# Interleaving two hidden units of a dense layer with chunk attention on one Trainium2 core

## Chip, cores and metric

The kernel runs on one core of one Trainium2 chip. The metric is the time of one execution on the device in microseconds (us), as the median of several runs. Before the change three runs took 1961.25, 1962.05 and 1965.11 us.

## What is computed

Three stages follow each other. Everything is float32; only shapes and the operations matter here.

```python
# 1. chunk attention: batch 4, heads 8, sequence 576, head size 64, chunks of 64
scores = q_c @ k_c.T / sqrt(64); attn = softmax(scores); x = attn @ v_c
x = x.transpose(0, 2, 1, 3).reshape(2304, 512)
# 2. dense layer ("first layer"): w_in 512x2048, w_out 2048x512 (float64 inputs)
h = x @ w_in; g = s * relu(h)**2 + b; x = g @ w_out
# 3. mixture of 8 experts with a doubly normalised gate
P = exp(x @ w_gate - max); P = normalise rows and columns of P, 8 times
out = sum over e of P[:, e] * (relu(x @ w1[e]) @ w2[e])
```

## The kernel before

**Tokens.** The 2304 tokens are 18 tiles of 128, numbered from 0, in 6 groups of 3 tiles (`GT`). Attention works by tile. The first layer works by group, so its products have 384 columns.

**Attention.** `attn_stages(t)` is a generator with five steps for a tile t. Step 0 transposes q and k on TensorE (banks `pq`, `pk`; 4 transposes each), ScalarE copies them to `qT` and `kT`, and the loads of tile t + 3 are issued on SyncE's queue. Step 1 makes the scores (`sc`, two banks, 32 small matmuls); VectorE takes the row maximum (`mx`) and subtracts it (into `pr`, or into spare room of the tile `whole`). Step 2 is the softmax: ScalarE's exp (L284), three VectorE instructions for the reciprocal of the row sums (`sm`, L286 to L288), and GpSimd's product (L289). Step 3 transposes the result (`pa`), and ScalarE copies it to `aT`. Step 4 multiplies by v (`px`, two banks); ScalarE writes the high part `xTh` of the layer's input and VectorE the low part `xTl`; the v of tile t + 2 is loaded. `attention()` runs the steps as a pipeline over tiles: in one round tile r has step 0, tile r - 2 step 2, tile r - 1 step 1, tile r - 3 step 3 and tile r - 4 step 4. A call of `stage()` advances it by one step (step 2 comes along with the next).

**First layer.** The 2048 hidden columns are 8 units of 256. For unit u and group g, `up1(u, g)` makes h: for each of two halves f, 12 matmuls of 128x384 into a bank `ph` (`three` sums high x high, high x low and low x high over 4 blocks of rows). ScalarE then does relu to `r` (L359), VectorE squares (L361), ScalarE writes the high part `gh` (L365), and VectorE the low part `gl` (L340), which `later()` puts off by one half. `down1(u, g)` makes the unit's share of the output: 4 slices of 6 matmuls into banks `po`. For unit 0 ScalarE copies the slice to the accumulator (L390); for other units VectorE adds it (L392). I write U(u, g) and D(u, g) for the two. All PSUM banks come from one ring of 8, in the order of the code.

**Weights.** They are float64 in memory, and are rounded to float32 and split on the chip, in blocks of 512 KB: a unit has blocks 4u and 4u + 1 (w_in) and 4u + 2 and 4u + 3 (w_out). `convert(i)` is two ScalarE instructions on the raw words (L189, L190), three on VectorE (L191, L193, L197) and two on GpSimd (L200, L201). `finish(i)` merges on VectorE (L208), writes the high part `wh` on ScalarE (L213) and the low part `wl` on GpSimd (L214). The generator `unit_conversion` alternates: convert(i), then finish(i - 1) with the load of raw block i + 1. There are two raw buffers (blocks 2 and 3 lie in spare room). Unit u's weights lie in a buffer of the pools `wpa` or `wpb`, by turns.

**Order.** The code writes the order out by hand, and each engine takes its own instructions in that order. While attention runs, unit 0 alone is interleaved with it: three attention steps stand behind each product slice (`stage(3)`), and as many as are missing stand ahead of each group (`while done[0] < ...: stage()`). The rest of unit 0's conversion is written in one piece behind U(0, 0). D of a group is written behind U of the next. When attention is through, the remaining slices of unit 0 and then units 1 to 7 follow, with the next unit's conversion beside each.

```python
                if u == 0:
                    while done[0] < G0[g] + GT[g]:
                        stage()
                    side = lambda: stage(3)
```

## Time and profile before

| what | value |
|---|---|
| three runs | 1961.25, 1962.05, 1965.11 us; median 1962.05 |
| span of the profiled execution | 1964.4 us; of the three runs only the one of 1965.11 us is longer |
| TensorE busy | 1917.2 us, 98% of the span |
| VectorE, ScalarE, GpSimd busy | 1377.4, 982.9, 156.4 us |
| TensorE busy in the first three of 40 slices | 6, 8 and 8 tenths; GpSimd works in the first ten slices only |

TensorE is busy nearly all the time, so most of the time is work that the change leaves alone. Attention and most of unit 0 lie in the first 127 us. Within that stretch one reads the idle time of TensorE, what ended it, and the granted clock.

### The profile page before, as it was taken

How to read it: one execution, taken by the hardware profiler on the slowest of the kernel's cores; microseconds unless marked ns; L12 is line 12 of the kernel's file. 1: busy time of each engine (PE TensorE's matmuls, PEld its weight loads, DVE VectorE, ACT ScalarE, POOL GpSimd, SP SyncE). 2: the span in 40 equal slices, each digit the busy share in tenths (PEclk: the TensorE clock that was granted, in tenths of full speed). 3: DMA queues.
4: the chain of work that ended last, by engine and by line, in shares of the span. 5: the costliest groups of instructions: out<-in, count | busy, mean ns of one | idle time of the engine just before them, and what ended most of it. 6: DMA issues, size and time to landing. Idle time of an engine off the chain costs nothing.

```text
span 1964.4 us, 34768 instructions
## 1 busy us (share of the span) xinstructions
PE 1917.2 (98%) x13859; PEld 1889.7 (96%) x13859; DVE 1377.4 (70%) x2417; ACT 982.9 (50%) x1793; POOL 156.4 (8%) x126
## 2 busy tenths in 40 slices
PE   6889999999899999999999999999999999999999
PEld 5779999999799999999999999999999999999998
DVE  5666777775767666656665666888887878788775
ACT  4664333335544445454545444555555555555553
POOL 4333333330000000000000000000000000000000
PEclk9899999999999999999999999999999999999999
DMA  8521111100155565556555656867676766767675
GB/s 193 144 65 43 44 44 43 44 22 12 39 201 212 197 227 220 205 204 225 222 204 205 225 222 226 295 188 226 178 229 189 224 200 205 223 190 226 180 228 168
DMA packets 295729, 335.71 MB, mean 171 GB/s; under 512 B 65936, under 2 KB 254352, under 8 KB 295568
## 3 DMA queue, kind: packets, MB, share of 16 engines
q1 hardware_dynamic: 295568, 333.50, 52.1%
q8 instruction: 108, 1.77, 0.4%
q14 instruction: 53, 0.43, 0.1%
HBM read 196.63 MB, written 136.84 MB: 170 GB/s over the span
## 4 chain that ended last, share of the span: by engine, by line
PE 90%; DVE 4%; ACT 3%; issue 1%; DMA 1%; POOL 0%; SPq 0%; DVEq 0%; ACTq 0%; POOLq 0%
PE wb L612 71%; PE ph L107 9%; PE po L107 9%; DVE sm L286 0%; DMA vs<-in_v_dram 0%; DVE mx L279 0%; ACT whole L660 0%; DVE whole L280 0%; DVE x L521 0%; ACT r L369 0%; DMA whole<-in_q_dram 0%; PE px L304 0%; ACT r L359 0%; DVE xs L524 0%; ACT r L368 0%
## 5 line engine op out<-in xcount | busy, mean ns | idle before, releaser
L612 PEld LDWEIGHTS wb<-x,x 128*128 128x128 f32 x6048 | 726.1, 192 | 2.4 <-ACT wb L850 2.2
L612 PE MATMUL wb<-x,x 128*128 128x256 f32 x6048 | 726.8, 283 | 1.5 <-ACT wb L850 1.5
L612 PE MATMUL wb<-x,w1h 128*128 128x384 f32 x2688 | 686.8, 337 | 6.9 <-ACT w1h L572 2.2
L612 PEld LDWEIGHTS wb<-x,w1h 128*128 128x128 f32 x2688 | 484.5, 188 | 10.1 <-ACT wb L687 3.2
L612 PE MATMUL wb<-x,w1l 128*128 128x384 f32 x1344 | 451.8, 336 | 0.1
L817 DVE TENSOR_TENSOR x<-st,x 128x1024 fp32r<-128x1024 f32 (+1 forms) x288 | 308.3, 1089 | 101.7 <-ACT x L816 100.3
L816 ACT ACTIVATE x<-st 128x1024 fp32r<-128x1024 f32 (+1 forms) x288 | 272.1, 945 | 111.3 <-issue 79.4
L612 PEld LDWEIGHTS wb<-x,w1l 128*128 128x128 f32 x1344 | 252.7, 188 | 0.4 <-DVE w1l L574 0.4
L844 DVE SCALAR_TENSOR_TENSOR whole<-wb,lg,whole 128x256 f32<-128x256 f32 (+1 forms) x333 | 166.0, 530 | 49.2 <-PE wb L612 46.7
L850 ACT ACTIVATE wb<-wb 128x256 f32<-128x256 f32 x216 | 79.4, 368 | 233.1 <-PE wb L612 221.8
L675 DVE SCALAR_TENSOR_TENSOR whole<-wb,whole 128x384 f32<-128x384 f32 x192 | 98.1, 552 | 126.8 <-PE wb L612 105.4
L660 ACT ACTIVATE whole<-whole 128x384 f32<-128x384 f32 x192 | 100.2, 527 | 156.1 <-DVE whole L666 118.5
L107 PE MATMUL po<-gh,wh 128*128 128x384 f32 x384 | 130.8, 341 | 1.4 <-ACT whole L390 0.8
L107 PE MATMUL ph<-xTh,wh 128*128 128x384 f32 x384 | 130.1, 339 | 0.8 <-ACT xTh L312 0.8
L107 PE MATMUL ph<-xTl,wh 128*128 128x384 f32 x384 | 129.4, 337 | 1.3 <-DVE xTl L313 1.3
L107 PE MATMUL ph<-xTh,wl 128*128 128x384 f32 x384 | 129.4, 337 | 0.0
L107 PE MATMUL po<-gl,wh 128*128 128x384 f32 x384 | 128.9, 336 | 0.0
L107 PE MATMUL po<-gh,wl 128*128 128x384 f32 x384 | 128.8, 335 | 0.0
L361 DVE SCALAR_TENSOR_TENSOR r<-r,s_bc 128x384 f32<-128x384 f32 x84 | 64.7, 770 | 75.4 <-ACT r L359 75.4
L574 DVE TENSOR_TENSOR w1l<-w,w1h 128x512 fp32r<-128x512 f32 (+1 forms) x128 | 79.0, 620 | 34.3 <-ACT w1h L572 34.3
L365 ACT ACTIVATE gh<-r,b_bc 128x384 fp32r<-128x384 f32 x84 | 51.9, 617 | 82.6 <-DVE r L361 82.6
L692 ACT ACTIVATE whole<-wb 128x384 f32<-128x384 f32 x96 | 47.4, 494 | 91.2 <-PE wb L612 91.1
(133 smaller groups left out, 1974.1 us busy)
## 6 DMA issues: line engine op xcount, KB each, us to landing
h<-whole SPq DMA_DIRECT2D x96, 1344.0 KB, 5.7
st<-h SPq DMA_DIRECT2D x216, 512.0 KB, 4.5
w<-in_moe_w_dram SPq DMA_DIRECT2D x60, 512.0 KB, 6.8
st<-h SPq DMA_DIRECT2D x72, 256.0 KB, 4.3
raw<-in_moe_w_in_dram SPq DMA_DIRECT2D x16, 512.0 KB, 3.6
raw<-in_moe_w_out_dram SPq DMA_DIRECT2D x14, 512.0 KB, 3.5
vs<-in_v_dram SPq DMA_DIRECT2D x72, 64.0 KB, 2.6
out_dram<-whole SPq DMA_DIRECT2D x18, 256.0 KB, 3.9
```

The costliest lines, as they stand in the source:

```text
L107: nc.tensor.matmul(out, lhsT=x, rhs=y, start=(i == 0), stop=(i == n - 1))
L361: nc.vector.scalar_tensor_tensor(out=r, in0=r, scalar=s_bc[:, 0:1], in1=r, op0=ALU.mult, op1=ALU.mult)
L365: nc.scalar.activation(out=hh, in_=r, func=AF.Identity, bias=b_bc[:, 0:1])
L574: nc.vector.tensor_tensor(out=dst(lo), in0=src, in1=dst(hi).bitcast(F32), op=ALU.subtract)
L612: nc.tensor.matmul(out, lhsT=x, rhs=y, start=fresh and i == 0, stop=i == n - 1, skip_group_check=True)
L660: nc.scalar.activation(out=dst, in_=src, func=AF.Relu)
L675: nc.vector.scalar_tensor_tensor(out=dst, in0=view(b), scalar=0.0, in1=y, op0=ALU.max, op1=op)
L692: nc.scalar.activation(out=u2, in_=b, func=AF.Copy)
L816: nc.scalar.activation(out=h, in_=src, func=AF.Copy)
L817: nc.vector.tensor_tensor(out=l, in0=src, in1=h.bitcast(F32), op=ALU.subtract)
L844: nc.vector.scalar_tensor_tensor(out=dst, in0=src, scalar=g, in1=dst, op0=ALU.mult, op1=ALU.add)
L850: nc.scalar.activation(out=dst, in_=src, func=AF.Copy)
```

## The change

- Units 0 and 1 both run on a group as it leaves attention. The order of the slices is now a list (`steps`): U(0,0), D(0,0), U(0,1), U(1,0), D(0,1), U(0,2), D(1,0), U(1,1), D(0,2), U(0,3), D(1,1) and so on, to D(1,4); D(1,5) follows with unit 2.
- Attention steps are spread evenly: 12 between two groups, over the slices that lie there (`pending`): two steps behind each slice of the first group, later one.
- Blocks 0 to 11 (units 0 to 2) are converted beside attention, at places that a table (`turns`) names by slice. Behind the first half of U(0,0) it has two turns in one: finish(2) with the load of raw block 4, and convert(4).
- D(0,0) comes directly behind U(0,0); `flush()` writes the low parts that it needs ahead of it.
- The weight buffers are opened once. A third one (`wc`) holds the w_in part of units 2 and 5, and is closed ahead of unit 6.
- Units 2 to 7 run as before.

```diff
--- before.py
+++ after.py
@@ -59,6 +59,8 @@
     xp = [None] * NG
     for g in reversed(range(NG)):
         xp[g] = open_pool(x_stacks[g], f"xp{g}")
+    third = ExitStack()
+    wc = open_pool(third, "wc", bufs=2)
     cv = open_pool(early, "cv", side="right")
     at = open_pool(early, "at", bufs=2, side="right")
     ffn_banks = ExitStack()
@@ -136,10 +138,15 @@
                 )
 
 
+    pairs = [[p.tile([P, 2, KD * UN], F32R, tag="w", name=f"w{x}{i}") for x in "hl"]
+             for i, p in enumerate(wp)]
+    ups = [[t[:, 0] for t in both] for both in pairs]
+    ups.append([wc.tile([P, KD * UN], F32R, tag="w", name=f"wc{x}") for x in "hl"])
+    dns = [[t[:, 1] for t in both] for both in pairs]
+
     def part_tiles(u):
-        both = [wp[u % 2].tile([P, 2, KD * UN], F32R, tag="w", name=f"w{x}{u}") for x in "hl"]
-        up = [t[:, 0].rearrange("p (k f) -> p k f", k=KD) for t in both]
-        dn = [t[:, 1].rearrange("p (k f) -> p k f", k=UF) for t in both]
+        up = [t.rearrange("p (k f) -> p k f", k=KD) for t in ups[u % 3]]
+        dn = [t.rearrange("p (k f) -> p k f", k=UF) for t in dns[u % 2]]
         return up, dn
 
     units = []
@@ -213,9 +220,8 @@
         nc.scalar.activation(out=dh, in_=m, func=AF.Copy)
         nc.gpsimd.tensor_tensor(out=dl, in0=m, in1=dh.bitcast(F32), op=ALU.subtract)
 
-    def unit_conversion(first):
-
-        n = len(conv)
+    def conversion(first, n):
+
         load_raw(first)
         load_raw(first + 1)
         yield
@@ -886,7 +892,8 @@
         load_qk(0)
         make_identity(nc, ident)
         nc.gpsimd.memset(ones, 1.0)
-        plan_unit(0)
+        for u in range(NU1):
+            plan_unit(u)
         load_raw(0)
         load_qk(1)
         load_raw(1)
@@ -913,7 +920,7 @@
                 if x is not None:
                     done[0] = x
 
-        cg = unit_conversion(0)
+        cg = conversion(0, 12)
         next(cg)
         i = 0
         while done[0] < GT[0]:
@@ -922,7 +929,59 @@
             stage()
             i += 1
         stage(2)
-        prev = None
+
+        def flush():
+            while lows:
+                later()
+
+        steps = [("U", 0, 0), ("D", 0, 0), ("U", 0, 1), ("U", 1, 0), ("D", 0, 1), ("U", 0, 2), ("D", 1, 0)]
+        for g in range(1, NG - 2):
+            steps += [("U", 1, g), ("D", 0, g + 1), ("U", 0, g + 2), ("D", 1, g)]
+        steps += [("U", 1, NG - 2), ("D", 0, NG - 1), ("U", 1, NG - 1), ("D", 1, NG - 2)]
+        by = {}
+        for j, (what, u, g) in enumerate(steps):
+            if u == 0 and (what, g) in [("U", x) for x in range(NG)] + [("D", NG - 2)]:
+                by.setdefault(NG - 1 if what == "D" else g, j)
+        turns = {("U", 0, 0): (2, 1), ("D", 0, 0): (1, 0, 1, 0), ("U", 0, 1): (1, 1), ("U", 1, 0): (1, 0),
+                 ("D", 0, 1): (1, 0, 1, 0), ("U", 0, 2): (1, 0), ("U", 0, 3): (1, 0), ("U", 0, 4): (1, 0),
+                 ("U", 1, 3): (1, 0), ("D", 0, 5): (0, 0, 0, 1), ("U", 1, 5): (1, 1), ("D", 1, 4): (1, 0, 0, 0)}
+        taken_hs = {}
+        pending = []
+
+        def paced(counts):
+            counts = list(counts)
+
+            def side():
+                for _ in range(counts.pop(0)):
+                    next(cg, None)
+                if pending:
+                    stage(pending.pop(0))
+            return side
+
+        marks = sorted((j, g) for g, j in by.items())
+        for j, (what, u, g) in enumerate(steps):
+            for at_, g_ in marks:
+                if at_ == j:
+                    while done[0] < G0[g_] + GT[g_]:
+                        stage()
+                    later_marks = [a for a, _ in marks if a > j]
+                    if later_marks:
+                        n = sum(2 if w == "U" else 4 for w, _, _ in steps[j:later_marks[0]])
+                        pending[:] = [12 * (x + 1) // n - 12 * x // n for x in range(n)]
+                    else:
+                        pending[:] = [9] * 2
+            side = paced(turns.get((what, u, g), (0,) * 4))
+            if what == "U":
+                taken_hs[u, g] = up1(u, g, side)
+            else:
+                if (u, g) == (0, 0):
+                    flush()
+                down1(u, g, taken_hs.pop((u, g)), side)
+        prev = 1, NG - 1, taken_hs.pop((1, NG - 1))
+        for _ in att:
+            pass
+        for _ in cg:
+            pass
         bx = []
 
         def last_side():
@@ -930,38 +989,22 @@
             if bx:
                 next(bx[0], None)
 
-        for u in range(NU1):
-            if u:
-                if u + 1 < NU1:
-                    plan_unit(u + 1)
-                if u + 1 < NU1:
-                    cg = unit_conversion(4 * (u + 1))
-                else:
-                    early.close()
-                    cg = first_weights()
-                next(cg)
+        for u in range(2, NU1):
+            if u + 1 < NU1:
+                cg = conversion(4 * (u + 1), 4 * (u + 2))
+            else:
+                early.close()
+                cg = first_weights()
+            if u == NU1 - 2:
+                third.close()
+            next(cg)
             for g in range(NG):
-                if u == 0:
-                    while done[0] < G0[g] + GT[g]:
-                        stage()
-                    side = lambda: stage(3)
-                elif u == NU1 - 1:
-                    side = last_side
-                else:
-                    side = idle
-                if u or g:
+                side = last_side if u == NU1 - 1 else idle
+                next(cg, None)
+                hs = up1(u, g, side)
+                if g:
                     next(cg, None)
-                hs = up1(u, g, side if u else lambda: stage(3))
-                if u == 0 and g == 0:
-                    for _ in cg:
-                        pass
-                    plan_unit(1)
-                    cg = unit_conversion(4)
-                    next(cg)
-                elif u == 0 or g:
-                    next(cg, None)
-                if prev is not None:
-                    down1(*prev, side)
+                down1(*prev, side)
                 prev = u, g, hs
                 if u == NU1 - 1:
                     x_stacks[g].close()
```

Three places of the order. Line numbers behind the change are higher by 6 or 7. First ScalarE, from the first relu on, before (`r_0_0` is the relu of U(0,0), half 0; `pr` and `whole` with no other operand are the exps of tiles 3 and 4; `qT`, `kT` belong to tile 6):

```order
L359 ACTIVATE r_0_0_546<-ph_0_0_531 128x384
L365 ACTIVATE gh_0_0_544<-r_0_0_546,b_bc 128x384
L284 ACTIVATE pr<-pr 128x512
L253 ACTIVATE qT_586<-pq_581 128x512
L259 ACTIVATE kT_593<-pk_588 128x512
L284 ACTIVATE whole<-whole 128x512
L359 ACTIVATE r_0_1_641<-ph_0_1_626 128x384
L365 ACTIVATE gh_0_1_639<-r_0_1_641,b_bc 128x384
```

and now (`wh` is the split of blocks 2 and 3, `raw_560` is block 4, which SyncE's queue now loads right behind q and k of tile 8):

```order
L365 ACTIVATE r_0_0_553<-ph_0_0_538 128x384
L371 ACTIVATE gh_0_0_551<-r_0_0_553,b_bc 128x384
L220 ACTIVATE wh_116<-whole 128x512
L196 ACTIVATE m_562<-raw_560 128x512
L197 ACTIVATE l_564<-raw_560 128x512
L290 ACTIVATE pr<-pr 128x512
L259 ACTIVATE qT_608<-pq_603 128x512
L265 ACTIVATE kT_615<-pk_610 128x512
L365 ACTIVATE r_0_1_634<-ph_0_1_619 128x384
L371 ACTIVATE gh_0_1_632<-r_0_1_634,b_bc 128x384
L220 ACTIVATE wh_116<-whole 128x512
L290 ACTIVATE whole<-whole 128x512
```

Ahead of the exp of tile 3 and of everything behind it now stand the split of block 2 and the two instructions that read block 4.

Second, VectorE behind U(0,0)'s second half, before:

```order
L361 SCALAR_TENSOR_TENSOR r_0_1_641<-r_0_1_641,s_bc 128x384
L340 SCALAR_TENSOR_TENSOR gl_0_0_545<-r_0_0_546,b_bc,gh_0_0_544 128x384
L286 TENSOR_REDUCE sm_670<-whole 128x8
L287 TENSOR_SCALAR sm_670<-sm_670 128x8
L288 RECIPROCAL sm_670<-sm_670 128x8
L279 TENSOR_REDUCE mx_693<-sc_0_675 128x4
```

and now (L215 is the merge of block 3; `sm_645` belongs to tile 4 and `sc_0_650`, `sc_1_651` to tile 5):

```order
L367 SCALAR_TENSOR_TENSOR r_0_1_634<-r_0_1_634,s_bc 128x384
L346 SCALAR_TENSOR_TENSOR gl_0_0_552<-r_0_0_553,b_bc,gh_0_0_551 128x384
L215 SCALAR_TENSOR_TENSOR whole<-whole 128x512
L292 TENSOR_REDUCE sm_645<-whole 128x8
L293 TENSOR_SCALAR sm_645<-sm_645 128x8
L294 RECIPROCAL sm_645<-sm_645 128x8
L285 TENSOR_REDUCE mx_668<-sc_0_650 128x4
L286 TENSOR_TENSOR whole<-sc_0_650,mx_668 128x4x64
L285 TENSOR_REDUCE mx_668<-sc_1_651 128x4
L286 TENSOR_TENSOR whole<-sc_1_651,mx_668 128x4x64
L346 SCALAR_TENSOR_TENSOR gl_0_1_633<-r_0_1_634,b_bc,gh_0_1_632 128x384
```

The low part `gl_0_1` of U(0,0) now stands behind the softmax sums of tile 4 and the scores of tile 5, and TensorE's first slice of D(0,0) reads it; that slice stands behind the scores of tile 5 and the transposes of tile 3.

Third, VectorE ahead of U(0,2), before (`xTl_580` is the low part of group 1, `xTl_822` that of group 2):

```order
L313 TENSOR_TENSOR xTl_580<-px_0_1190,xTh_579 128x4x64
L313 TENSOR_TENSOR xTl_580<-px_1_1191,xTh_579 128x4x64
L286 TENSOR_REDUCE sm_1241<-whole 128x8
L287 TENSOR_SCALAR sm_1241<-sm_1241 128x8
L288 RECIPROCAL sm_1241<-sm_1241 128x8
L279 TENSOR_REDUCE mx_1264<-sc_0_1246 128x4
L280 TENSOR_TENSOR pr<-sc_0_1246,mx_1264 128x4x64
L279 TENSOR_REDUCE mx_1264<-sc_1_1247 128x4
L280 TENSOR_TENSOR pr<-sc_1_1247,mx_1264 128x4x64
L313 TENSOR_TENSOR xTl_822<-px_0_1284,xTh_821 128x4x64
L313 TENSOR_TENSOR xTl_822<-px_1_1285,xTh_821 128x4x64
```

and now (`xTl_602` is that of the group that U(0,2) reads; `r_2_0` is its first half):

```order
L292 TENSOR_REDUCE sm_1285<-whole 128x8
L293 TENSOR_SCALAR sm_1285<-sm_1285 128x8
L294 RECIPROCAL sm_1285<-sm_1285 128x8
L285 TENSOR_REDUCE mx_1308<-sc_0_1290 128x4
L286 TENSOR_TENSOR whole<-sc_0_1290,mx_1308 128x4x64
L285 TENSOR_REDUCE mx_1308<-sc_1_1291 128x4
L286 TENSOR_TENSOR whole<-sc_1_1291,mx_1308 128x4x64
L319 TENSOR_TENSOR xTl_602<-px_0_1328,xTh_601 128x4x64
L319 TENSOR_TENSOR xTl_602<-px_1_1329,xTh_601 128x4x64
L367 SCALAR_TENSOR_TENSOR r_2_0_1369<-r_2_0_1369,s_bc 128x384
```

The low part of a group's third tile is now the last thing ahead of the products that read it; TensorE has `px` of that tile directly ahead of them, at U(0,1), U(0,2) and U(0,3). Before, that was so at U(0,1) alone.

## Rows read from the trace of the kernel before

**Rows 1.** Page: the span, and the engines busy over it.
```profile
span 1964.4 us, 34768 instructions
...
PE 1917.2 (98%) x13859; PEld 1889.7 (96%) x13859; DVE 1377.4 (70%) x2417; ACT 982.9 (50%) x1793; POOL 156.4 (8%) x126
```

**Rows 2.** Page: the chain that ended last, shares by engine.
```profile
PE 90%; DVE 4%; ACT 3%; issue 1%; DMA 1%; POOL 0%; SPq 0%; DVEq 0%; ACTq 0%; POOLq 0%
```

**Rows 3.** Windows: length; PE, PEld, DVE, ACT, POOL busy; clock; DMA share; GB/s.
```profile
36.30:63.20 26.90, 19.86 (x328) 16.53 (x327) 15.99 (x42) 14.69 (x31) 7.04 (x7) 0.87 0.73 175
63.20:90.87 27.67, 24.36 (x392) 21.13 (x392) 20.44 (x52) 17.54 (x38) 10.19 (x9) 0.94 0.55 124
90.87:127.38 36.51, 29.80 (x515) 25.61 (x508) 26.93 (x65) 22.43 (x51) 11.73 (x10) 0.99 0.39 96
36.30:166.29 129.99, 112.93 (x1445) 102.18 (x1445) 83.45 (x190) 76.01 (x160) 40.59 (x34) 0.95 0.41 98
```

**Rows 4.** Chain in order of time: U of unit 1, 24 matmuls.
```profile
166.29 4.16 PE ph L107 x24
```

**Rows 5.** Windows of 5 us, columns as in rows 3.
```profile
45.00:50.00 5.00, 2.39 (x73) 1.85 (x71) 3.56 (x9) 2.05 (x5) 1.04 (x1) 1.00 0.80 199
50.00:55.00 5.00, 2.74 (x51) 2.05 (x45) 3.73 (x9) 1.61 (x4) 1.16 (x2) 0.99 0.73 203
55.00:60.00 5.00, 3.80 (x52) 3.16 (x56) 2.63 (x8) 4.74 (x12) 3.06 (x3) 0.50 0.43 96
```

**Rows 6.** Timeline of TensorE: start, us, instruction [idle before <-releaser].
```profile
43.94 0.66 PE L294 MATMUL pa<-ident,pr 128*128 128x128 f32 x4 [0.20 <-POOL pr L289]
...
63.20 0.44 PE L107 MATMUL ph<-xTh,wh 128*128 128x384 f32 x1 [0.77 <-ACT xTh L312]
...
64.91 0.51 PE L107 MATMUL ph<-xTl,wh 128*128 128x384 f32 x1 [1.26 <-DVE xTl L313]
```

**Rows 7.** Timeline of ScalarE behind the first half of U(0,0).
```profile
39.19 0.49 ACT L359 ACTIVATE r<-ph 128x384 f32<-128x384 f32 x1 [2.20 <-PE ph L107]
40.37 0.61 ACT L365 ACTIVATE gh<-r,b_bc 128x384 fp32r<-128x384 f32 x1 [0.69 <-DVE r L361]
40.89 0.61 ACT L284 ACTIVATE pr<-pr 128x512 f32<-128x512 f32 x1
```

**Rows 8.** Timeline of SyncE's DMA queue: the last load of tile 8.
```profile
38.76 0.80 SPq L120 DMA_DIRECT2D whole<-in_k_dram  x1
```

**Rows 9.** Tile raw, 0 to 170 us: time from issue to landing.
```profile
DMA to landing us min/median/max: 3.5/4.8/6.4
```

**Rows 10.** Waits of ScalarE, 50 to 58 us: total, times, longest.
```profile
ACT wh L213 <- DVE whole L208: 3.4, 1, 3.4
```

**Rows 11.** Timeline of VectorE, one row for each kind of work.
```profile
41.54 0.69 DVE L286 TENSOR_REDUCE sm<-pr 128x8 f32<-128x512 f32 x1 [1.20 <-ACT pr L284]
...
42.59 0.37 DVE L279 TENSOR_REDUCE mx<-sc 128x4 f32<-128x256 f32 x1
...
43.78 0.42 DVE L280 TENSOR_TENSOR whole<-sc,mx 128x256 f32<-128x256 f32 x1
...
47.56 0.61 DVE L361 SCALAR_TENSOR_TENSOR r<-r,s_bc 128x384 f32<-128x384 f32 x1
...
53.47 1.28 DVE L208 SCALAR_TENSOR_TENSOR whole<-whole 128x512 uint32<-128x512 uint32 x2
...
60.61 0.74 DVE L313 TENSOR_TENSOR xTl<-px,xTh 128x256 fp32r<-128x256 f32 x2
...
65.68 0.43 DVE L197 TENSOR_SCALAR e<-m 128x512 uint32<-128x512 uint32 x1
```

**Rows 12.** Timeline of GpSimd: a softmax product and a conversion.
```profile
42.84 1.04 POOL L289 TENSOR_TENSOR pr<-pr,sm 128x512 f32<-128x512 f32 x1 [6.99 <-DVE sm L288]
...
66.28 1.27 POOL L200 TENSOR_TENSOR l<-l,e 128x512 f32<-128x512 f32 x1 [2.41 <-DVE e L197]
67.63 1.27 POOL L201 TENSOR_TENSOR m<-l,m 128x512 f32<-128x512 f32 x1
```

## The prediction

> **What bounds the kernel now.** I read the page first: TensorE is busy for 1917.2 of the span's 1964.4 us [rows 1], and 90% of the chain that ended last is TensorE's [rows 2]. A change of order can gain only where TensorE idles or runs at the lower clock. The windows say where. From the first product of U(0,0) at 36.30 to 166.29, 130.0 us, TensorE is busy for 112.9, so 17.1 us are idle, and the mean granted clock is 0.95 [rows 3]. The fall itself is in the 5 us windows: with TensorE busy 2.39 and 2.74 of 5 us between 45 and 55 the clock is still 1.00 and 0.99, and in the next window it is 0.50, the lower level of 1.2 GHz [rows 5]. 0.05 of 130 us is 6.5 us of lost pulses, a bit less where TensorE idled anyway. So some 23 us are there to be won. At 166.29 stands the U of group 2 in unit 1 [rows 4]. In TensorE's order that U has the same row number before and after (703), and from there both run the same slices in the same order; TensorE is dense before (24 matmuls in 4.16 us, 173 ns each [rows 4]). So **the question is when this row starts now**, and the difference goes into the end one for one.
>
> Idle TensorE alone doesn't say that more products would fill it. VectorE is busy 15.99, 20.44 and 26.93 us in the three windows of 26.90, 27.67 and 36.51 us, 59% and then 74% [rows 3]: it is the second engine, takes its work in order, and so does ScalarE. Where one of them waits, all behind waits: ScalarE's split of a weight block stood 3.4 us for VectorE's merge [rows 10].
>
> **The change, part by part.** The matmuls up to row 703 are the same, 360 of the products and the same attention. VectorE's conversions are nearly the same too: 6 converts and 7 finishes before, 14 turns now. The third weight buffer adds no work; it only allows the w_in part of unit 2 early, and what used to be converted beside dense products later was hidden there, so I cost its absence there at nothing. More changes between attention and products cost TensorE a little: in the third window 72 product matmuls (12.5 us) and 5.7 tiles' worth of attention fill 29.8 us less 0.6 of slow clock, so a tile costs 2.9 us with its changes [rows 3]. With some 16 more changes at 0.13 us (an estimate from the 20 to 30 in these windows) I add 2 us.
>
> What decides is the order on ScalarE and VectorE. I follow it with the trace's durations: on VectorE a tile's softmax sums take 1.05 us (41.54 to 42.59), the evacuation of its scores 1.6 (42.59 to 44.20), a square or a low part 0.55, a merge 0.64 (two in 1.28), the two low parts of x 0.74, a conversion 1.3 (three of 0.43) [rows 11]; on GpSimd a product 1.04 and a convert 2.6 [rows 12]; on ScalarE some 0.55 an instruction [rows 7].
>
> *Stage A, to the first product of U(0,1).* Block 4 is loaded right behind tile 8's k, issued at 38.76 for 0.80 us [rows 8], so its own issue starts near 40. These loads land in 3.5 to 6.4 us, median 4.8 [rows 9]; I take the median, 45.0, since tiles 7 to 9 are loading too. ScalarE has done relu, `gh` and block 2's split by 41.7 and then stands 3.3 us for block 4. The exp of tile 3, begun at 40.89 before [rows 7], begins at 46.1. VectorE: block 4 to 47.0, sums to 48.05. GpSimd takes block 4 first (to 49.65), then tile 3's product, ready at 50.7. TensorE has done all else by 43.7 (before, tile 3's transposes began at 43.94 after a wait of only 0.20 [rows 6]) and idles 7.0 us. Then D(0,0): its fifth matmul reads `gl_0_1`, which on VectorE stands behind tile 4's scores (to 49.65), square, low part and merge (51.45), an exp that waits on ScalarE behind the split of block 3 (52.7), sums and scores of tile 5 (55.4): 55.95. TensorE idles another 2.9. With this much idle the clock falls, as it did with half as much work [rows 5]. The rest of D(0,0) with four rounds of attention then goes at the pace of exp to sums to scores: the sums of tiles 5, 6 and 7 begin at 60.1, 66.3 and 70.0, and tile 5's low part is ready at 73.4, with another 2.6 idle. **U(0,1) starts in earnest at 73.4**, before at 64.91 [rows 6], but with D(0,0) done, 24 matmuls or 4.2 us.
>
> *Stage B, U(0,1), U(1,0), D(0,1) and three tiles.* TensorE has 72 x 0.173 + 3 x 2.9 + 1 = 22 us of work, VectorE 20. Four waits come out of the same walk: tile 8's transposes for a PSUM bank until tile 6's low part is read (1.2), tile 12's for one until tile 10's scores are read (1.8), tile 11's scores for one that `aT` is copied from (1.1), and U(0,2) for tile 8's low part (5.4), because ScalarE stands for the merge of block 6 and for raw block 8. Together 9.5 us: **U(0,2) at 105.5**.
>
> *Stage C, to row 703.* 240 matmuls (41.6), 7.2 tiles (20.9), 2.4 for more changes, 2.5 of waits (1 of them at U(0,3)): VectorE has 45 us of work in it, two thirds, and keeps up. 67.4 us, so 172.9.
>
> **Sum.** 172.9 against 166.29: 6.6 us slower. Or by idle time: 12.5 + 9.5 + 2.5 = 24.5 against 17.1, plus 2 us for changes, less some 3 us of slow clock in stage A against 6 in all before, again 6 to 7. I take 6.8. The profiled execution's own time is 1965.1 by the only run longer than its span; the median is 3.1 below, and the forecast is made on the median: 1962.05 + 6.8 = 1968.9 us.
>
> Here the Trainium skill speaks: "DMA: Bandwidth & Descriptors", section "Anatomy of one DMA", fits a transfer as 2.0 us and bytes over 436e3, an estimate of 3.2 us for 512 KB, for GpSimd's path. No row is as short (3.5 at least [rows 9]); by the page block 4 would land 1.6 us earlier, and the sum would be 1967.3.
>
> **Bounds.** Landing of block 4: 3.5 us takes 1.3 off, 6.4 adds 1.6. Clock: the waits ahead of U(0,1) and U(0,2) are like the one at 63.20, whose first products ran at the lower clock afterwards; 12 matmuls at twice 0.173 add 2 us each; none in the sum. Waits of stage C: none to 6 us, by the 3.3 and 6.7 us idle in the second and third window [rows 3].
>
> **Rivals.**
> *VectorE keeps pace* (faster). The walk leaves VectorE 65% busy from 55.95 to U(0,2), where 32.2 us of its work lie; before, it reached 74% [rows 3]. If the spread steps let it fill to 90%, U(0,2) starts at 91.8, TensorE's own work (34 us with the slow start) allows it, and row 703 is at 159.2, 7.1 earlier: 1955.0 us. It decides from 83% on: below that the gain is under 4 us. For it: products between the steps give every step time, and the stretch from 45 to 55, where TensorE is half idle with nothing but attention to do, is gone. Against it: no window before comes near [rows 3].
> *Even.* VectorE runs at the 74% of before; U(0,2) at 99.5, row 703 at 166.9: 1962.7 us. What was idle between groups is idle ahead of D(0,0) and U(0,2) instead.
> *Slower, more of it.* The forecast with both falls of the clock and a late block: 1968.9 + 4 + 1.6 = 1974.5; part of the forecast's own range, 1966 to 1975.
>
> **Chances.** Forecast 0.58, even 0.24, faster 0.18. 0.2%, about 4 us, is what a measurement of this kernel can tell from no change (the three runs span 3.9). So faster by more 0.18, within 0.24, slower 0.58. The range takes in the fast rival's price and the bounds on the slow side: 1955 to 1976.
>
> **What would show it.** Right: ScalarE's first instruction on raw block 4 waits for its DMA by about 3 us near 42 to 45; TensorE idles some 7 us ahead of tile 3's transposes and 3 in D(0,0)'s first slice; the product slices from U(0,2) on have idle time of 2 to 3 us in all; the U at row 703 starts near 173. Wrong: tile 3's transposes follow before 46, or U(0,2) starts before 98. The time is faster if VectorE is over 83% busy up to U(0,2).

## The result, and the profile after

The changed kernel takes **1986.79 us** (median of 4 runs, 1982.14 to 1989.36) against 1961.7 (4 runs). The ratio is 1.0119, 95% interval 1.0102 to 1.0136. The forecast was 1968.9 with a range to 1976: the sign is right and the size is not.

The page of the changed kernel (profiled execution, 1989.09 us) answers to [rows 1] and [rows 2]: TensorE is busy 11.8 us longer with the same 13859 instructions, and it carries 87% of the chain instead of 90.

```profile
span 1987.3 us, 34752 instructions
...
PE 1929.0 (97%) x13859; PEld 1897.5 (95%) x13859; DVE 1382.7 (70%) x2417; ACT 983.5 (49%) x1793; POOL 155.8 (8%) x126
...
PE 87%; DVE 4%; ACT 3%; DMA 1%; issue 1%; POOL 0%; SPq 0%; ACTq 0%; DVEq 0%
```

To see where the time went I cut both executions at the same points of TensorE's order: the first product of U(0,0), the first of U(2,0), the first of U(3,0), and 90 us from the same matmul on in the passage to the experts. Windows of the kernel before and of the changed one, columns as in [rows 3]:

```profile
35.95:199.41 163.46, 146.40 (x1638) 135.65 (x1637) 107.25 (x232) 89.75 (x186) 51.92 (x41) 0.96 0.36 91
199.41:249.33 49.92, 49.92 (x289) 49.92 (x289) 36.41 (x66) 19.52 (x36) 17.26 (x12) 1.00 0.13 43
489.41:579.41 90.00, 82.30 (x471) 75.22 (x471) 63.20 (x110) 49.84 (x92) 0.00 (x0) 1.00 0.32 115
```

```profile
36.47:214.57 178.10, 152.78 (x1639) 139.11 (x1638) 106.48 (x227) 87.45 (x182) 46.70 (x39) 0.90 0.32 77
214.57:266.98 52.41, 50.74 (x290) 49.78 (x289) 40.22 (x67) 20.80 (x39) 21.63 (x15) 1.00 0.19 61
507.06:597.06 90.00, 82.00 (x441) 75.77 (x441) 60.70 (x103) 47.07 (x86) 0.00 (x0) 0.94 0.27 99
```

The spans differ by 22.9 us: 0.5 before U(0,0), **14.6 in the early stretch** (units 0 and 1 with attention), **2.5 in unit 2**, and **5.2 behind it** (1987.3 - 266.98 against 1964.4 - 249.33). In the early stretch TensorE idles 25.3 us instead of 17.1, and the same products and attention keep it busy 6.4 us longer, at a mean clock of 0.90 instead of 0.96.

The first wait is the one that was forecast. ScalarE, in order, stands 3.9 us for raw block 4, and tile 3's exp (L290) stands behind it and starts at 46.65 instead of 40.89 [rows 7]:

```profile
45.54 0.66 ACT L196 ACTIVATE m<-raw 128x512 f32<-128x512 f32 x1 [3.91 <-DMA raw<-in_moe_w_in_dram]
...
46.65 0.62 ACT L290 ACTIVATE pr<-pr 128x512 f32<-128x512 f32 x1
```

TensorE's waits (its timeline) follow from there: tile 3's transposes (0.20 before [rows 6]), D(0,0)'s low part, U(0,1), U(1,0)'s second half for block 5's split, and U(0,2):

```profile
51.45 1.11 PE L300 MATMUL pa<-ident,pr 128*128 128x128 f32 x4 [7.89 <-POOL pr L295]
...
57.40 0.69 PE L109 MATMUL po<-gl,wh 128*128 128x384 f32 x1 [3.05 <-DVE gl L346]
...
74.69 0.58 PE L109 MATMUL ph<-xTl,wh 128*128 128x384 f32 x1 [1.96 <-DVE xTl L319]
...
86.94 0.44 PE L109 MATMUL ph<-xTh,wh 128*128 128x384 f32 x1 [1.58 <-ACT wh L220]
...
111.27 0.69 PE L109 MATMUL ph<-xTl,wh 128*128 128x384 f32 x1 [2.34 <-DVE xTl L319]
```

And the clock, in windows of 5 us (compare [rows 5]): 0.50 behind the first wait, 0.68 in the first products of U(0,1), 0.50 in those of U(0,2), where 12 matmuls take 3.73 us, 311 ns each against 173 [rows 4].

```profile
50.00:55.00 5.00, 2.76 (x8) 1.85 (x8) 3.72 (x8) 2.25 (x4) 2.67 (x3) 0.50 0.00 0
...
75.00:80.00 5.00, 5.00 (x24) 4.91 (x24) 0.62 (x1) 0.85 (x2) 0.00 (x0) 0.68 0.75 161
...
110.00:115.00 5.00, 3.73 (x12) 3.64 (x13) 1.18 (x4) 0.00 (x0) 1.09 (x2) 0.50 0.08 17
```

### The profile page after: what moved, and what is told of

Read it like the earlier page. It is cut to its first block, busy times and chain, and to the rows that moved or that the text cites. A ratio compares the mean times of both kernels' runs of the same rounds, so it can differ in the third digit from the quotient of the medians.

```text
span 1987.3 us, 34752 instructions
## 1 busy us (share of the span) xinstructions
PE 1929.0 (97%) x13859; PEld 1897.5 (95%) x13859; DVE 1382.7 (70%) x2417; ACT 983.5 (49%) x1793; POOL 155.8 (8%) x126
## 4 chain that ended last, share of the span: by engine, by line
PE 87%; DVE 4%; ACT 3%; DMA 1%; issue 1%; POOL 0%; SPq 0%; ACTq 0%; DVEq 0%
PE wb L618 70%; PE ph L109 8%; PE po L109 8%; DVE r L367 1%; DVE gl L346 0%; DMA raw<-in_moe_w_in_dram 0%; DMA st<-h 0%; ACT r L365 0%; DMA raw<-in_moe_w_out_dram 0%; ACT whole L666 0%; DVE x L527 0%; ACT r L375 0%; ACT m L196 0%; PE px L310 0%; DVE m L215 0%
## 5 line engine op out<-in xcount | busy, mean ns | idle before, releaser
L618 PEld LDWEIGHTS wb<-x,w1h 128*128 128x128 f32 x2688 | 487.5, 189 | 10.8 <-ACT wb L693 3.2
L109 PE MATMUL ph<-xTh,wh 128*128 128x384 f32 x288 | 99.7, 346 | 4.9 <-ACT xTh L318 3.3
L109 PE MATMUL ph<-xTl,wh 128*128 128x384 f32 x288 | 98.8, 343 | 4.4 <-DVE xTl L319 4.3
L109 PE MATMUL ph<-xTh,wl 128*128 128x384 f32 x288 | 98.6, 342 | 0.7 <-POOL wl L221 0.7
```

What stands on the lines that cost most here:

```text
L109: nc.tensor.matmul(out, lhsT=x, rhs=y, start=(i == 0), stop=(i == n - 1))
L618: nc.tensor.matmul(out, lhsT=x, rhs=y, start=fresh and i == 0, stop=i == n - 1, skip_group_check=True)
```

## The experiments

Each row is one kernel: the median, its ratio to the kernel before on the same chip, and from its profiled execution the early stretch (first product of U(0,0) to first of U(2,0)), TensorE's clock in it, unit 2, and the rest. Code behind unit 2 is the same in all. The start of U(0,0) lay between 32.3 and 36.5 us, in kernels that do the same up to there too, so lengths are compared and not moments.

Lengths have limits of their own. There is one profiled execution of each kernel, and the same code does not always take the same time in it: from D(1,2) to the next slice it is 8.7 us in after and 7.1 to 9.1 in e1 to e6, whose instructions there are after's, as the clock falls in it or not. And block 4's load is issued at 39 to 42 us in all versions of the change, wherever U(0,0) starts, so a kernel whose ScalarE waits for it gains nothing by an early start, and its stretch only looks longer: in e4 U(0,0) starts 3.6 us sooner than in after, ScalarE waits 7.4 us for block 4 instead of 3.9, and U(0,1) starts in earnest at 75.0 us instead of 74.7. A difference of some 2 us between two stretches is therefore no result by itself; the medians stand beside them. The kernel before, run again with each group, had medians of 1961.7 to 1965.6.

| kernel | median us | ratio (95%) | early us | clock | unit 2 | rest |
|---|---|---|---|---|---|---|
| before | 1961.7 | 1 | 163.5 | 0.96 | 49.9 | 1715.1 |
| after | 1986.8 | 1.0119 (1.0102-1.0136) | 178.1 | 0.90 | 52.4 | 1720.3 |
| e1 block 4 later | 1980.1 | 1.0079 (1.0060-1.0098) | 174.2 | 0.91 | 52.5 | 1715.2 |
| e2 D(0,0) behind U(0,1) | 1982.7 | 1.0091 (1.0074-1.0109) | 177.9 | 0.91 | 52.4 | 1716.1 |
| e3 blocks 4, 8 later | 1978.7 | 1.0071 (1.0056-1.0086) | 173.8 | 0.92 | 52.6 | 1717.4 |
| e4 one filler | 1985.1 | 1.0107 (1.0088-1.0126) | 178.9 | 0.94 | 52.7 | 1717.6 |
| e5 four fillers | 1982.6 | 1.0097 (1.0080-1.0115) | 175.0 | 0.96 | 52.4 | 1716.8 |
| e6 e2 and e3 | 1978.4 | 1.0072 (1.0055-1.0089) | 172.2 | 0.95 | 52.4 | 1717.0 |
| e7 e3, turns earlier | 1977.4 | 1.0065 (1.0050-1.0080) | 172.8 | 0.95 | 49.9 | 1720.1 |
| e8 unit 1 later | 1977.4 | 1.0066 (1.0050-1.0083) | 175.9 | 0.94 | 49.9 | 1716.0 |
| e9 e6, group 2 sooner | 1971.7 | 1.0047 (1.0029-1.0065) | 166.5 | 0.96 | 52.5 | 1716.5 |
| e10 e6, all blocks later | 1981.7 | 1.0098 (1.0081-1.0115) | 168.7 | 0.95 | 58.4 | 1715.4 |
| e11 e9 and e10 | 1973.2 | 1.0052 (1.0037-1.0067) | 168.4 | 0.94 | 53.6 | 1715.5 |
| e12 blocks 4-7 left out | 1963.8 | 1.0003 (0.9993-1.0012) | 159.4 | 0.96 | 52.6 | 1715.3 |
| e13 e9, unit 2's turns | 1968.0 | 1.0022 (1.0009-1.0035) | 167.3 | 0.95 | 49.9 | 1715.6 |
| e14 e13, block 4 after U(0,1) | 1973.4 | 1.0039 (1.0024-1.0054) | 170.1 | 0.96 | 49.9 | 1715.5 |
| e15 e14, D(0,1) first | 1969.5 | 1.0024 (1.0014-1.0035) | 166.0 | 0.95 | 49.9 | 1718.1 |
| e16 e13 and fillers | 1967.8 | 1.0014 (1.0006-1.0023) | 165.0 | 0.98 | 49.9 | 1717.1 |
| e17 e15's order, e13's blocks | 1967.8 | 1.0013 (1.0004-1.0022) | 165.8 | 0.95 | 49.9 | 1717.1 |
| e18 e17 and fillers | 1966.6 | 1.0010 (1.0001-1.0018) | 163.3 | 0.98 | 49.9 | 1715.6 |

**One wait at a time (e1, e2, e3).**

```diff
 for i in range(first + 1, n):            # e1: at = {4}; e3: at = {4, 8}
-    convert(i); yield
+    if i not in at: convert(i); yield
     finish(i - 1); load_raw(i + 1); yield
+    if i in at: convert(i); yield
```
```diff
-steps = [("U",0,0), ("D",0,0), ("U",0,1), ...     # e2
+steps = [("U",0,0), ("U",0,1), ("D",0,0), ...
```

> Only the order of two turns is changed: block 3 is finished and block 5 loaded before block 4 is converted, so ScalarE reads block 4 one product slice later. Theory (waits in the in-order queues): the 7.9 us that TensorE idled ahead of tile 3's transposes fall below 2.5 us, the clock stays up there, and the time falls by 8 to 13 us from the changed kernel's 1986.8. Rival (VectorE is simply full until U(0,2)): the gap only moves to D(0,0) or U(0,1), and the time stays within 4 us of 1986.8.

> Only D(0,0) is moved behind U(0,1), as in the kernel before; block 4 stays where the change put it. Theory: the 3.0 us wait of D(0,0)'s first slice for the low part goes, the 7.9 us ahead of tile 3's transposes stay: 2 to 4 us off 1986.8. Rival (TensorE lacks work among the first tiles): with six attention steps behind each half of U(0,0) the idle time there grows, and the time rises by 2 to 6 us.

> As the first, and block 8 also converted one turn later, behind U(0,2)'s first half instead of inside D(0,1). Theory: ScalarE no longer stands 3.9 us for block 8's transfer ahead of the exp of tile 10, U(0,2) starts 3 to 5 us earlier than in the first, and the time is 3 to 5 us below the first's. Rival (VectorE is full): U(0,2) starts where it did in the first, and the time is within 2 us of it.

With block 4 later, tile 3's transposes wait 2.2 us instead of 7.9, and D(0,0)'s low part 7.0 instead of 3.0. e3's timeline of TensorE shows the same pair:

```profile
42.82 0.66 PE L304 MATMUL pa<-ident,pr 128*128 128x128 f32 x4 [2.20 <-POOL pr L299]
...
52.15 0.69 PE L109 MATMUL po<-gl,wh 128*128 128x384 f32 x1 [6.62 <-DVE gl L350]
```

So raw block 4 does cause the first wait, but most of that wait only moved to the next slice that reads from the crowded engines; 3.9 us of the early stretch were gained, 1.6 of them in D(1,2), where e1 changes nothing. The median fell by 6.7 us, more than the rival's 4 and less than the theory's 8 to 13. In e2 the wait moved the other way: the transposes wait 11.4 us, and the early stretch is as long as before the edit. Its median is 4.1 us lower, about as the theory said, but in the profile 4.2 us lie behind unit 2, where the code is the same. Block 8 later takes 2.9 us off the way from U(0,0) to U(0,2) in e3 against e1, but only 0.5 off the stretch and 1.4 off the median, within the rival's 2.

**The clock (e4, e5).** Added matmuls that nobody reads, at the places of the waits.

```diff
+def extra(n, tag):                        # 128x384 into a bank of its own
+    for x in range(n): nc.tensor.matmul(junk, lhsT=uh[...], rhs=xT[0][0][...], ...)
+extra(40) ahead of pa3                    # e4 and e5
+extra(14) ahead of D(0,0), 14 ahead of U(0,1), 20 ahead of U(0,2)    # e5
```

> The changed kernel with 40 extra matmuls of 128x384 ahead of tile 3's transposes, into a bank that nothing reads: 6.9 us of work at the full clock into a wait of 7.9 us. It measures the clock alone. If the lower clock behind that wait costs what its windows show (granted 0.50 from 50 to 60 us with 5.4 us of work in it), the clock stays at 1.00 there and 2 to 4 us come off 1986.8. If the clock costs nothing because TensorE waits anyway, the time is within 1.5 us of 1986.8. The waits themselves stay.

> This kernel adds 88 matmuls of 128x384 whose results nobody reads (40 ahead of tile 3's transposes, 14 ahead of D(0,0), 14 ahead of U(0,1), 20 ahead of U(0,2)), each lot shorter than the wait that stands there in the changed kernel (7.9, 3.0, 2.8 and 4.1 us) when a matmul takes 0.16 us. Theory (the clock that falls behind the waits is the larger part of what I left out): the granted clock from 36.3 us to row 703 rises from 0.88 to 0.95 or more, the first products of U(0,1) and U(0,2) run at 173 ns instead of twice that, and the product that stood in row 703 starts 6 to 9 us earlier than 181.4, at 172 to 175; the median is 1978 to 1981. Rival (the clock falls where TensorE would idle anyway, and VectorE and ScalarE set the pace): row 703's product starts at 179 to 184 whatever the clock, and the median stays within 4 us of 1986.8.

e4 held the clock up to 50 us. Because of its longer wait for block 4, 4.2 us of idle time were left behind the fillers; the clock is 0.73 from 50 to 55 us and 0.50 from 55 to 60, and the median is 1.7 us lower, between the two expectations. So e4 decides little. e5 is the cleaner test, since U(0,0) starts at 36.3 there and at 36.5 in after. Its windows, the early stretch first:

```profile
36.34:211.30 174.96, 162.88 (x1726) 149.93 (x1725) 106.47 (x227) 86.84 (x182) 46.79 (x39) 0.96 0.32 79
...
75.00:80.00 5.00, 4.97 (x31) 4.79 (x31) 0.98 (x2) 2.06 (x4) 0.00 (x0) 1.00 0.63 126
110.00:115.00 5.00, 4.88 (x31) 4.81 (x31) 1.28 (x3) 1.95 (x4) 0.15 (x1) 1.00 0.00 0
```

Each lot left 0.4 to 1.9 us of its wait, so the fillers themselves held nothing up. The clock is that of the kernel before, 0.96, and the products of U(0,1) and U(0,2) run at full clock. Yet the stretch is only 3.1 us shorter, and U(0,1) and U(0,2) start nearly where they did (75.0 and 110.1). The theory's 6 to 9 us fall; the rival is nearer (4.2 us under the changed kernel instead of within 4). The clock is a part of the loss, by this test the smaller one.

**The conversions taken out (e12).**

```diff
+left_out = (4, 5, 6, 7)     # load_raw, convert and finish return at once for these
+for i in left_out: for half in conv[i][1]: nc.vector.memset(half, 0.37)
```

> The changed kernel without the load, convert and finish of blocks 4 to 7: unit 1's weights are constants written once at the start, all slices and all attention stay. It leaves out 4 x 1.9 us of VectorE, 4 x 1.8 of ScalarE and 4 x 4.1 of GpSimd ahead of U(0,2). Theory (these conversions, in order among the attention's work, are what TensorE waits for): tile 3's transposes wait 1 us or less, D(0,0) 1 or less, U(0,1) runs in earnest at 60 to 64 instead of 74.7, U(0,2) at 85 to 90 instead of 111.3, the first U of unit 2 at 188 to 193 instead of 214.6; the median is 1961 to 1966. Rival (the attention's round through the engines, with more slices between its steps, is what takes the time): U(0,1) at 66 to 70, U(0,2) at 98 to 104, the first U of unit 2 at 200 to 208, the median at 1973 to 1980.

```profile
36.12:195.54 159.42, 145.95 (x1639) 133.64 (x1637) 94.59 (x211) 81.25 (x170) 31.06 (x27) 0.96 0.31 73
```

The stretch falls by **18.7 us**, from 178.1 to 159.4, with the change's order of slices and attention untouched. VectorE has 11.9 us less to do, ScalarE 6.2, GpSimd 15.6: the gain is more than any one engine's work that went, which fits engines that stand in order behind one another. (The loads of these blocks are gone too, so e12 does not part the work from the waits for loads.) U(0,1) runs in earnest at 68.0 and U(0,2) at 94.4, later than the theory's 60 to 64 and 85 to 90, and U(2,0) at 195.5 lies between the two expectations: attention's own round takes a share, but the four blocks are the larger cause. (That median is no gain to be had, since unit 1's weights must be converted.)

**The order around them (e6, e9, e8).** e6 joins e2 and e3; e9 issues group 2's attention one slice sooner; e8 lets unit 1 follow two groups behind unit 0.

```diff
+by[2] -= 1        # e9: the mark of group 2 at D(0,1) instead of U(0,2)
```

> Both earlier edits together: blocks 4 and 8 converted one turn later, and D(0,0) behind U(0,1). Theory (ScalarE and VectorE, in order, carry the waits: block 4 holds tile 3's exp, and D(0,0) reads a low part queued behind attention): tile 3's transposes wait 2 to 4 us instead of 7.9, D(0,0) waits for no low part, U(0,1) starts in earnest at 62 to 66, U(0,2) by 99 and row 703 at 167 to 171: 1970 to 1975. Rival (the attention of group 1 alone takes until 69, whatever stands beside it; both edits only move idle time): U(0,1) at 67 to 70 as in either edit alone, row 703 at 173 to 176, 1977 to 1980.

> As the run with D(0,0) behind U(0,1) and blocks 4 and 8 later, and group 2's attention is issued one slice sooner, done ahead of D(0,1) instead of ahead of U(0,2). Theory (from U(0,1) to U(0,2) TensorE waits for the attention of group 2, whose steps stand too far apart in its order: 4.8 us ahead of U(0,2) there): that wait falls under 1.5 us, U(0,2) runs in earnest at 97 to 99 instead of 102.3, the first U of unit 2 at 200 to 202 instead of 204.9, the median at 1973 to 1976 against 1978.4. Rival (attention takes its time on VectorE and ScalarE; issued sooner it only waits sooner, now with D(0,1) behind it): the wait stands ahead of D(0,1) instead, U(0,2) at 101 to 104, the median at 1977 to 1980.

> Unit 1 enters two groups later: U(0,1), D(0,0), U(0,2), D(0,1) in the order of the kernel before, and from then on unit 1 runs two token groups behind unit 0; blocks 4 and 8 one turn later, the turns spread over the later slices. Theory (the loss is in what unit 1's conversion and slices do to groups 1 and 2, and the gain of the change is there from group 3 on, where VectorE has time): U(0,1) and U(0,2) start as before, at 65 and 91 to 93; the idle of some 9 us that the kernel before has from 98 to 130 falls to 2 to 4; the first U of unit 2 (199.5 before, 214.7 after) starts at 192 to 196, and the time is 4 to 7 us under the kernel before: 1956 to 1960. Rival (attention's round through VectorE sets the pace of every group, whatever products stand between): the idle comes back beside groups 3 to 5, the first U of unit 2 at 198 to 203, 1962 to 1967.

In e6 the two edits work together: D(0,0) no longer waits for a low part, and U(0,1) runs in earnest 29.4 us behind the start of U(0,0), nearly as early as in the kernel before (29.0, from 35.95 to 64.91 [rows 6]; 38.2 in after). The next stop takes most of it back, and the median is the rival's (TensorE's timeline of e6):

```profile
62.13 0.69 PE L109 MATMUL ph<-xTl,wh 128*128 128x384 f32 x1 [1.95 <-DVE xTl L323]
...
102.29 0.44 PE L109 MATMUL ph<-xTh,wh 128*128 128x384 f32 x1 [4.77 <-ACT xTh L322]
```

e9 removes that wait by order alone. U(0,2) starts at 99.8 without one, and the early stretch is 5.7 us shorter than e6's and **11.6 shorter than after's**, with all its work kept (the medians are 6.7 and 15.1 us lower). So what the four blocks cost depends on what stands behind them. e8 fell: U(0,2) came at 89.8, but group 3's attention was now spread over the slices from U(0,2) to D(0,2), and U(0,3) came at 127.2. In e7 and e8 blocks 10 and 11 are merged into unit 0's down weights before D(0,5) has read them, so D(0,5) multiplies by weights of unit 2.

**Unit 2 (e7, e10, e11, e13).** In the changed kernel ScalarE waits for raw blocks 14 and 15 ahead of the relu of U(2,2) and U(2,3), one block per 10.0 us against 8.3 us of products, and D(2,2) and D(2,3) wait for low parts. Timeline of ScalarE, waits of TensorE from 241 to 272 us, and the loads of 228 to 260 us:

```profile
237.60 0.66 ACT L196 ACTIVATE m<-raw 128x512 f32<-128x512 f32 x1 [2.87 <-DMA raw<-in_moe_w_out_dram]
...
247.61 0.67 ACT L196 ACTIVATE m<-raw 128x512 f32<-128x512 f32 x1 [2.92 <-DMA raw<-in_moe_w_out_dram]
```
```profile
PE po L109 <- DVE gl L346: 1.7, 3, 0.8
```
```profile
raw<-in_moe_w_out_dram SPq DMA_DIRECT2D x2, 512.0 KB, 3.4
```

The kernel before has these ScalarE waits too and no TensorE wait. e7 and e13 move the last turns of blocks 9 to 11 up; e10 turns the order of convert and merge round for all blocks from 4 to 15.

```diff
-("U",0,4): (1,0), ("U",1,3): (1,0), ("D",0,5): (0,0,0,1), ("U",1,5): (1,1), ("D",1,4): (1,0,0,0)
+("U",1,2): (1,0), ("U",0,4): (1,0), ("U",1,3): (1,0), ("U",0,5): (1,0),     # e13, on e9
+("D",0,5): (0,0,0,1), ("U",1,5): (1,0)
```

> Blocks 4 and 8 one turn later as in the run with both, and the turns of blocks 9 to 11 spread so that none is left for D(0,5), U(1,5) and D(1,4). Theory (in the part behind row 703 the 1.7 us of waits for low parts in unit 2 come from conversions of blocks 10 and 11 that stand right ahead of those of 12 to 15): these waits fall to 0.3 us or less, and the time is 1.5 us under the run with both blocks later, 1977.2. Rival (unit 2's own conversions, one block per 10 us against 8.3 us of products, make the lag by themselves): 1.7 us stays, 1978.7 plus or minus 1; or the turns crowd VectorE earlier and row 703 comes 1 to 2 us later.

> As the run with D(0,0) behind U(0,1), and every block from 4 to 15 is converted one turn later, behind the merge of the block before it and the load of the block behind it. Theory (ScalarE's waits for raw blocks, 4.6, 2 and 3.9 us in the changed kernel and 2.9 us twice in unit 2, come from a load that is issued one turn ahead of its use): ScalarE waits under 1 us in all for raw blocks 4 to 15, unit 2's 1.7 us of waits for low parts go, U(0,2) comes at 99 to 101 instead of 102.3, and the median is 1974 to 1977. Rival (the raw blocks are not what ends last; the merges now stand ahead of the converts and wait for GpSimd instead): the waits of TensorE keep their sum within 1.5 us and the median is 1977 to 1980.

> Both of these together, and block 10's convert moved up to U(1,3) and U(1,5) one turn lighter. Theory: both gains add, the first U of unit 2 at 198 to 200, as in the kernel before (199.5), no wait for low parts in unit 2, and the median at 1968 to 1972; it would beat the changed kernel by 15 to 19 us and still not the kernel before. Rival (attention sets the pace up to U(0,2) whatever is moved): 1975 to 1978.

> The best run so far (D(0,0) behind U(0,1), blocks 4 and 8 later, group 2's attention sooner), with the last turns of the early conversion moved up: block 11 is converted in U(0,5) and merged in U(1,5), nothing is left for D(1,4). Theory (unit 2 takes 52.4 us instead of 49.9 because blocks 10 and 11 run late into blocks 12 to 15 on ScalarE): unit 2 takes 49.9 to 50.3 us, no wait for a low part there, and the median is 2 to 3 us under that run's 1971.7: 1969 to 1970. Rival (the two transitions behind it, or unit 2's own cadence, take it back): 52 us, 1971 to 1973.

e13's unit 2 is the kernel before's again, and its median is 3.7 us under e9's (the profile gives 2.6 of that to unit 2):

```profile
200.42:250.34 49.92, 49.92 (x289) 49.92 (x289) 36.85 (x66) 19.53 (x36) 17.26 (x12) 1.00 0.14 43
```

So blocks 10 and 11, converted right ahead of 12 to 15, were the 2.5 us; e7, which moves them too, has the same 49.9 us. e10 is the warning: ScalarE's waits for raw blocks went, but its splits now stand ahead of the relu and wait for VectorE's merges, and unit 2 takes 58.4 us. GpSimd, which the rival named, ended one wait of a merge in unit 2, of 1.2 us; mostly the merges stand behind VectorE's own work. e11, which joins e9 and e10, has 53.6 us in unit 2 and a median between its two expectations. TensorE's and ScalarE's waits in e10 (205 to 330 us, and 36 to 262 us):

```profile
PE po L109 <- DVE gl L350: 6.8, 5, 1.9
```
```profile
ACT wh L220 <- DVE m L215: 32.3, 9, 4.7
```

**Level with the kernel before? (e14 to e18).** e14 and e15 begin blocks 4 and 5 beside U(0,1); e15 and e17 place U(1,0) behind D(0,1); e16 and e18 add 42 and 34 fillers.

```diff
-("D",0,0), ("U",1,0), ("D",0,1), ("U",0,2), ...      # e15, e17
+("D",0,0), ("D",0,1), ("U",1,0), ("U",0,2), ...
```

> The same, and blocks 4 and 5 are first touched beside U(0,1): one turn less beside U(0,0), one more beside D(0,0). Theory (every conversion ahead of U(0,1) delays group 1's attention): tile 3's transposes wait 1 to 3 us instead of 4.3, U(0,1) runs in earnest at 58 to 61 instead of 62.1, and that gain of 1 to 4 us is kept up to unit 2 (first U at 195 to 198 instead of 199.3): 1965 to 1968. Rival (U(1,0) then waits for block 5's split, as in the changed kernel): U(1,0) waits 2 us or more, first U of unit 2 at 199 to 201, 1969 to 1971.

> The same, and U(1,0) behind D(0,1), so that the blocks of unit 1 are spread over 4 us more. Theory (VectorE and ScalarE, filled with conversions between U(0,1) and U(0,2), are what attention waits for): the waits between U(0,1) and U(0,2) fall by 3 us or more, U(0,2) in earnest at 94 to 97 instead of 99.8, the first U of unit 2 at 192 to 196: 1962 to 1966, level with the kernel before. Rival (attention's own round is what is left): U(0,2) at 98 to 101, first U of unit 2 as in the run with blocks 4 and 5 beside U(0,1), or later by 1 to 3.

> The fastest version so far (group 2's attention sooner, unit 2's turns moved up, 1968.0) with 42 added matmuls of 128x384 whose results nobody reads: 22 ahead of tile 3's transposes (4.3 us of wait there), 12 ahead of U(0,1) (2.7 us) and 8 ahead of D(1,0) (1.8 us). Theory (where the order leaves few waits, the clock's falls behind them are what is left to be had): the granted clock between 60 and 70 us and between 110 and 115 us is 0.95 or more instead of 0.50 to 0.86 and 0.66, the first U of unit 2 comes 2 to 4 us earlier than 200.4, and the median is 1964 to 1966, level with the kernel before. Rival (as in the changed kernel with fillers, the engines beside TensorE set the pace and a higher clock mostly waits longer): first U of unit 2 at 199.5 to 201.5, 1967 to 1969.

> U(1,0) behind D(0,1) as in the run with that name, but blocks 4 to 7 converted in the places of the version with unit 2's turns moved up. In the former D(1,0) waited 4.0 us for the splits of blocks 6 and 7, and from the first product of U(0,0) to the first U of unit 2 it took 166.0 us (167.3 in the latter, 163.5 in the kernel before, 178.1 in the changed one). Theory (a block is free of cost where no slice waits for it and no attention stands behind it): these 4.0 us go and no other wait takes their place, 161 to 163.5 us, and the median is 1962 to 1965, level with the kernel before. Rival (the same conversions, sooner again, hold attention instead): 165 to 168 us, waits of 2 us or more ahead of U(1,0) or U(0,2), 1967 to 1970.

> The same with 34 added matmuls of 128x384 whose results nobody reads, 22 ahead of tile 3's transposes and 12 ahead of U(0,1), where TensorE waits 4.3 and 2.7 us. Theory (the clock's fall ahead of U(0,1) costs 2 us where little else waits: 167.3 became 165.0 with such fillers): 1.5 to 2.5 us less than without them in the stretch from U(0,0) to unit 2; the median 1 to 2 us lower. Rival: the stretch and the median as without them, within 0.7 us.

e14's stretch is 2.8 us longer than e13's, and its median lies above both expectations: the blocks left U(0,0) and came back between the starts of D(0,0) and U(1,0), 17.5 us instead of 12.9. e15's stretch is 4.1 us shorter than e14's, although D(1,0) now waited 4.0 us in all for blocks 6 and 7 (two of four rows of TensorE's timeline):

```profile
102.64 0.45 PE L109 MATMUL po<-gh,wh 128*128 128x384 f32 x1 [0.95 <-ACT wh L220]
...
106.43 0.69 PE L109 MATMUL po<-gh,wh 128*128 128x384 f32 x1 [2.00 <-ACT wh L220]
```

e17 took these waits away, and the stretch stayed at 165.8: the rival's number, though not the rival's waits (none of 2 us ahead of U(1,0) or U(0,2)). The trace shows where those 4 us went: U(0,2) starts 62.8 us behind U(0,0) instead of 59.8, with 1.0 us more idle time ahead of it and 2.1 us more busy time, at a clock of 0.86 instead of 0.91; whether the places of the blocks or chance brought these falls stays open. With fillers the stretch is 2.3 and 2.5 us shorter in e16 and e18 (3.1 in e5), and e18's is as long as before's; but the medians fell by 0.2 and 1.2 us only, and e16's is its rival's. e18's median lies 0.10% above, interval 0.01 to 0.18%. No version with the change's order beat the kernel before.

## Why the prediction was wrong, step by step

The forecast had U(2,0) 6.6 us later behind U(0,0) than before, 170.1 us; it is 178.1. Of the 22.9 us between the spans, 6.6 were in the sum and 16.3 were not. The three stages of the walk, up to U(0,1) in earnest, to U(0,2) in earnest and to row 703, show which term it was. Windows of the changed kernel, and the second stage in e5 (with 20 fillers in it):

```profile
36.47:74.69 38.22, 24.38 (x356) 20.56 (x354) 22.16 (x54) 19.51 (x40) 14.06 (x12) 0.82 0.54 127
74.69:111.27 36.58, 27.67 (x301) 24.15 (x301) 23.12 (x46) 17.96 (x38) 13.71 (x11) 0.83 0.50 118
111.27:181.28 70.01, 67.44 (x792) 61.11 (x793) 43.68 (x99) 35.20 (x75) 12.64 (x11) 0.94 0.24 58
```
```profile
75.03:110.12 35.09, 29.61 (x320) 26.17 (x320) 23.16 (x46) 17.93 (x38) 13.76 (x11) 0.90 0.47 112
```

| stage | length said, measured | idle said, measured | busy said, measured |
|---|---|---|---|
| A | 37.1, 38.2 | 12.5, 13.8 | 24.6, 24.4 |
| B | 32.1, 36.6 | 9.5, 8.9 | 22.6, 27.7 |
| C | 67.4, 70.0 | 2.5, 2.6 | 64.9, 67.4 |

- **The walk through stage A held.** ScalarE's stand for block 4: 3.3 said, 3.9 measured. Tile 3's transposes: 7.0 and 7.9. D(0,0)'s low part: 2.9 and 3.05. U(0,1) in earnest: 73.4 and 74.7. e1 shows that block 4 is the cause of the first of these waits. The load took up to 5.4 us (issued at 40.10, used at 45.54), beside attention's loads. The Trainium skill, "DMA: Bandwidth & Descriptors", "Anatomy of one DMA", gives an estimate of 3.2 us for its size, by GpSimd's path; the loads of blocks 14 and 15, alone on the queues, took 3.4, so the trace comes near it there and not here.
- **The idle time held, in stage B partly by luck.** 24.5 us said up to row 703, 25.3 measured. Of the four waits named for stage B, the one ahead of U(0,2) is there (5.4 said, 4.1 measured in two pieces) and the one of tile 11's scores (1.1 and 1.4), but tile 8's transposes do not wait and tile 12's wait 0.1 instead of 1.8. Block 5's split, 2.3 us in U(1,0)'s second half, was not in the walk and makes up for them.
- **"Clock: none in the sum" failed.** This is the step that cost most. U(0,2) came at 111.3, not 105.5, and the idle time does not tell it: the same work took longer, 27.7 us instead of 22.6 in stage B at a clock of 0.83, and 67.4 instead of 64.9 in stage C at 0.94. In the whole early stretch TensorE is busy 6.4 us longer than before. I had seen both places (the waits ahead of U(0,1) and U(0,2)), priced them at 2 us each and left them out. But the clock alone does not settle the miss either. With e5's fillers the stretch is 3.1 us shorter and U(0,2) starts only 1.0 us sooner behind U(0,0); stage B, at 0.90, is 35.1 us long, still 3.0 more than said. Whether full clock in all of it would take off these 3.0 us too, or other engines would end as many new waits, no run shows.
- **"So I cost its absence there at nothing" failed.** I looked at the dense products that used to hide blocks 8 to 11, and not at where their conversion ends now: right ahead of unit 2's own blocks. 2.5 us, shown by e13.
- **"The difference goes into the end one for one" failed by 5.2 us in the profiled execution.** (It failed in its reason too, at no cost: row 703 is U(1,3) now and not U(1,2), with D(0,4) and U(0,5) among the slices behind it; but they are as many, and U(2,0) starts 33.3 us behind row 703 in both.) At the passage to the experts the profile of after has 441 matmuls in 90 us at a clock of 0.94, where that of before has 471 at 1.00. The rest of the program took 1715 to 1720 us in the other kernels without relation to the edit, e7 and e13 included, whose unit 2 is the same. I take it for chance of the execution; that the change makes the fall likelier wasn't shown or excluded.
- **The reason given was half of it.** Order on ScalarE and VectorE was named as what decides, and e12 (18.7 us) with e9 (11.6 us by order alone) bear it out, both more than the noise of a stretch. That the interleaved products could win little I had argued from VectorE's share, 65% in the walk; the share came out as said (35.9 of 55.3 us from 55.95 to U(0,2)), and the rival with 90% was never near. In time, VectorE has 35.9 us of work there where the walk had 32.2. TensorE still idles 19.0 us in e13's early stretch (167.31 - 148.27), 17.1 in before's: the products of unit 1 stand between attention's steps, and the waits remain.

## What to carry to other kernels

A product slice placed between two dependent steps fills a wait only if the work that comes with it (here four weight conversions) doesn't enter the in-order queues that the wait is for; price the queues and then where the slice goes. When a wait is removed, look for the next reader of the same queue: in e1, e2, e6 and e10 the wait moved on and took part or all of the gain with it. And cost the end of the moved work too, where it runs into the next stage's own.
